# FNet and GeGLU block: the feature DFT for all tiles first, then the sequence DFT with its weights stationary, four of 16 chunks as block products

## Chip, cores and metric

One core of one Trainium2 chip. The metric is the device time in microseconds of one execution, as the median of several runs; 732.07 us for the kernel before (3 runs, 731.82 to 732.6).

## What is computed

```python
def _A_ref(x, dft_seq_re, dft_seq_im, dft_hid_re, dft_hid_im):
    a = jnp.einsum("bsd,ed->bse", x, dft_hid_re)
    b = jnp.einsum("bsd,ed->bse", x, dft_hid_im)
    y = jnp.einsum("ts,bse->bte", dft_seq_re, a) - jnp.einsum("ts,bse->bte", dft_seq_im, b)
    return y

def _B_ref(x, w_gate, w_up, w_down):
    g = jnp.einsum("bsd,df->bsf", x, w_gate)
    u = jnp.einsum("bsd,df->bsf", x, w_up)
    h = _gelu(g) * u
    return jnp.einsum("bsf,fd->bsd", h, w_down)

x = A_x
h = x + _A_ref(_layernorm(x, axis=-1), ...)
h2 = h + _B_ref(_layernorm(h, axis=-1), B_w_gate, B_w_up, B_w_down)
```

All tensors are fp32, with S = 2048 tokens, D = 448 features and 1792 hidden features; the batch is 1.

## The kernel before

Every fp32 operand of a matmul is split into two fp16 numbers, a hi half (rounded on ACT, `hi_part`, L105) and a lo half (the rest, on DVE, `lo_part`, L109 or L111). A product is three matmuls: hi x hi and the two mixed ones. TensorE has two sequencer records per matmul, the weight load (PEld: the stationary operand, 128 x 128) and the matmul (PE: the moving operand streams by, its columns are the width in the rows). PSUM has 8 banks of 512 fp32 columns.

The program has two stages, which run one after the other on PE.

*DFT stage.* It has 64 steps: 4 output blocks of 512 tokens (`b`) by 16 chunks of 128 input tokens (`c`). A tile of x is loaded (L340), normalised (`x_stats`, `x_norm`) and split (`xs`, kept on chip for all blocks). In a step `seq_mm` (L412) multiplies with the *x tile stationary* and the sequence DFT matrix `ws` moving, 512 columns: 2 parts (real, imaginary) x 3 feature slices x 3 terms = 18 matmuls into 6 banks; `seq_mm_rest` (L426) does the last 64 features of both parts in 6 half-width matmuls for a seventh bank. After 16 steps `z_out` splits the seven banks into `z`, and `hid_mm` (L477) applies the feature DFT: 4 token tiles x 7 slices x 3 terms = 84 matmuls of 448 columns; DVE adds x (L485) and gives `hx`, the h of the residual. For three blocks the `hid_mm` stand in between the steps of the next block; for the last they stand at its end. `w_seq` comes in 64 loads of 512 KB (L364), is split on ACT and DVE, five buffers ahead. In the same stage h of blocks 0 and 1 is normalised, split and transposed by DMA (`ffn_transpose`, L285) into `hops`, and the 14 gate/up weight blocks are summed, split (`class Weights`) and stored (`w_dram`, L333), the last three kept in a ring of buffers (`gw`).

*Gate/up and down stage.* 56 blocks of `GateUp` (L716, `product`, 256 columns, Strassen-like sums of operands) with the Gelu on ACT and products on POOL, and from block 14 on the down matmuls (L660, 224 columns). h of blocks 2 and 3 is prepared here. A last part does the remaining down matmuls without Gelu (L879, and L660 again).

The order is written out by hand and each engine runs its own file in that order: `early` and `after` hang work on a step of the DFT stage, `side` on a block of the second one. SP issues all DMAs in one file and waits there for what an issue needs.

Of the kernel before, what the change touches and what calls it, by code (L numbers as in the profile page):

```python
# [32 lines left out]
def kernel(  # L33
# [46 lines left out]
    ps_tr = ctx.enter_context(tc.tile_pool(name="ps_tr", bufs=1, space=bass.MemoryType.PSUM))  # L80
    right = ctx.enter_context(ExitStack())
    ps_seq = right.enter_context(tc.tile_pool(name="ps_seq", bufs=7, space=bass.MemoryType.PSUM))
# [6 lines left out]
    sign_t = const.tile([P, 1], F32, name="sign_t")  # L89
    G.memset(sign_t[:64], D_SC)  # L90
    G.memset(sign_t[64:], -D_SC)

# [4 lines left out]
    pw = ps_tr.tile([P, 8, P], F16, tag="tr", name="pw")  # L97
    for k in range(56):
        PE.transpose(pw[:, k % 8, :], ident, ident)  # L99
# [61 lines left out]
    def pair_tile(name):  # L161
        return ring.tile([P, 2, D], F32, tag="xh", bufs=5, name=name)

    def w_tile(name):
        return ring.tile([P, 28 * P], F16, tag="w", bufs=3, name=name)
# [125 lines left out]


    class Weights:


        def __init__(self, f):
            self.f = f
            self.raw = dft.tile([P, 2, 6, P], F32, tag="raw", bufs=2, name=f"gu_raw{f}")
            for r in range(2):
                nc.sync.dma_start(self.raw[:, r], w_gu[f, :, r])  # L300

        def sums(self):
            gate, up = self.raw[:, 0], self.raw[:, 1]
            s = self.s = dft.tile([P, 10, P], F32, tag="s", name=f"gu_s{self.f}")
            V.tensor_add(s[:, 0:3], up[:, 0:3], up[:, 3:6])
            V.tensor_sub(s[:, 3:6], s[:, 0:3], gate[:, 0:3])
            V.tensor_sub(s[:, 6:8], gate[:, 0:2], up[:, 0:2])
            V.tensor_sub(s[:, 8:10], gate[:, 4:6], s[:, 4:6])
# [15 lines left out]
        def split(self, of_raw):  # L324
            if of_raw:
                self.w = w_tile(f"gu_w{self.f}")
# [9 lines left out]
    xt, xs, norm_x = {}, {}, {}  # L336

    def x_load(i):
        xt[i] = dft.tile([P, 1, D], F32, tag="xt", bufs=3, name=f"x{i}")
        nc.sync.dma_start(xt[i][:, 0, :], x[i * P : (i + 1) * P, :])  # L340

    def x_stats(i):
        mv = stats(xt[i], f"x{i}")
        norm_x[i] = mv, root(mv, f"x{i}")

    def x_norm(i):
        mv, sd = norm_x.pop(i)
        xn = xt[i][:, 0, :]
        normed(xn, xn, mv, rstd(mv, sd, f"x{i}"), 0)
        xs[i] = dft.tile([P, 2, D], F16, name=f"xs{i}")  # L350
        hi_part(xs[i][:, 0], xn)

    def x_lo(i):
        lo_part(xs[i][:, 1], xt[i][:, 0, :], xs[i][:, 0])

    wr, ws = {}, {}

    def seq_load(n):
        wr[n] = dft.tile([P, 8 * P], F32, tag="wr", bufs=5, name=f"wr{n}")
        b, q, jj = n // NT, n // 2 % 8, n % 2
        nc.sync.dma_start(wr[n], w_seq[(2 * b + jj) * 8 + q])  # L364

    def seq_hi(n):
        if n % 2 == 0:
            ws[n // 2] = dft.tile([P, 2, 2, 8 * P], F16, tag="ws", bufs=4, name=f"ws{n // 2}")
        hi_part(ws[n // 2][:, 0, n % 2], wr[n], D_SC)

    def seq_lo(n):
        t = ws[n // 2][:, :, n % 2]
        lo_part(t[:, 1], wr[n], t[:, 0], D_SC)


    def first_load(c, jj):
        if c == 0:
            wr[jj] = dft.tile([P, 8 * P], F32, tag="wr", bufs=5, name=f"wr{jj}")
        if c == jj == 0:
            ws[0] = dft.tile([P, 2, 2, 8 * P], F16, tag="ws", bufs=4, name="ws0")  # L380
        cols = slice(c * P, (c + 1) * P)
        nc.sync.dma_start(wr[jj].rearrange("p (b t) -> p b t", b=4)[:, :, cols], w_seq[jj * 8][:, :, cols])

    def first_views(c, jj):
        cols = slice(c * P, (c + 1) * P)
        ts = [wr[jj], ws[0][:, 0, jj], ws[0][:, 1, jj]]
        return [t.rearrange("p (b t) -> p b t", b=4)[:, :, cols] for t in ts]

    def first_hi(c, jj):
        src, hi, lo = first_views(c, jj)  # L390
        hi_part(hi, src, D_SC)

    def first_lo(c, jj):
        src, hi, lo = first_views(c, jj)
        lo_part(lo, src, hi, D_SC)

    def seq_w(n, l, part):

        t = ws[n // 2][:, l].rearrange("p a (r g c t) -> p r c a g t", r=2, g=2, c=2)
        return t[:, part, n % 2]  # L400

    TERMS = ((0, 0), (1, 0), (0, 1))
    acc = {}

    def seq_mm(n, parts, terms=range(3)):

        b, c = divmod(n, NT)
        for part in parts:
            for k in range(3):
                for m in terms:  # L410
                    lx, lw = TERMS[m]
                    PE.matmul(  # L412
                        acc[b, 3 * part + k],
                        xs[c][:, lx, k * P : (k + 1) * P],
                        seq_w(n, lw, part),
                        start=c == 0 and m == 0,
                        stop=c == NT - 1 and m == 2,
                    )

    def seq_mm_rest(ns):  # L420

        for n in ns:
            b, c = divmod(n, NT)
            for m, (lx, lw) in enumerate(TERMS):
                for part in range(2):
                    PE.matmul(  # L426
                        acc[b, 6][64 * part : 64 * part + 64, :],
                        xs[c][:, lx, 3 * P :],
                        seq_w(n, lw, part),
                        start=c == 0 and m == 0,  # L430
                        stop=c == NT - 1 and m == 2,
                        skip_group_check=True,
                    )

    z = {}

    def z_out(b, k):
        if k == 0:
            z[b] = dft.tile([P, 2, 7, TB], F16, tag="z", name=f"z{b}")
        sc = 1.0 / (X_SC * D_SC)  # L440
        ps = acc.pop((b, k))
        hi_part(z[b][:, 0, k], ps, sc)
        lo_part(z[b][:, 1, k], ps, z[b][:, 0, k], sc)


    wh = dft.tile([P, 2, 7, D], F16, name="wh")
    wh_raw = {}

    def wh_load(g):

        t = wh_raw[g] = dft.tile([P, (3, 3, 1)[g], D], F32, tag="raw", bufs=2, name=f"wh_raw{g}")
        if g < 2:
            nc.sync.dma_start(t, w_hid[:, 0:3, g * D : (g + 1) * D])
        else:
            for r in range(2):
                nc.sync.dma_start(t[64 * r : 64 * r + 64, 0], w_hid[64 * r : 64 * r + 64, 3, r * D : (r + 1) * D])

# [683 lines left out]
```

## Time and profile before

| | us |
|---|---|
| median of 3 runs | 732.07 |
| profiled execution, span from first to last instruction | 730.1 |
| the runs' median less that span | 1.97 |
| first sequence matmul | 7.10 |
| first gate/up matmul | 364.91 |
| PE busy over the span | 718.5 |
| DVE, ACT, POOL busy | 523.0, 277.9, 242.1 |

The page holds one execution; its own time is the span beside what lies around it, which only the runs show. A row of a group reads: line, engine, operation, output <- input (partitions x elements, type) x count | busy us, mean ns of one | idle time of the engine just before, and what ended most of it. PE rows of a timeline include the pipelined end of the last matmul, so the distance of two starts, not the length of a row, is the price of what lies between; the pieces of the chain leave that end out.

### The profile page before, as it was taken

How to read it: one execution, taken by the hardware profiler on the slowest of the kernel's cores; microseconds unless marked ns; L12 is line 12 of the kernel's file. 1: busy time of each engine (PE TensorE's matmuls, PEld its weight loads, DVE VectorE, ACT ScalarE, POOL GpSimd, SP SyncE). 2: the span in 40 equal slices, each digit the busy share in tenths (PEclk: the TensorE clock that was granted, in tenths of full speed). 3: DMA queues.
4: the chain of work that ended last, by engine and by line, in shares of the span. 5: the costliest groups of instructions: out<-in, count | busy, mean ns of one | idle time of the engine just before them, and what ended most of it. 6: DMA issues, size and time to landing. Idle time of an engine off the chain costs nothing.

```text
span 730.1 us, 13452 instructions
## 1 busy us (share of the span) xinstructions
PE 718.5 (98%) x5309; PEld 497.9 (68%) x5309; DVE 523.0 (72%) x1071; ACT 277.9 (38%) x544; POOL 242.1 (33%) x281
## 2 busy tenths in 40 slices
PE   9999999999999999999999999999999999999987
PEld 5444444444444444444588889999999999999977
DVE  7888667486665866441377778787887877989794
ACT  4444703256233442311043444442444434454421
POOL 0000000000000001000057865576685867768360
PEclk9999999999999999999999999999999999999999
DMA  8667466577667976530057654747447676555311
GB/s 280 227 218 235 163 231 208 185 211 256 231 214 218 316 253 241 219 122 5 26 206 262 240 207 167 181 168 209 176 147 225 186 213 228 219 179 185 127 39 39
DMA packets 63503, 139.84 MB, mean 192 GB/s; under 512 B 30288, under 2 KB 39504, under 8 KB 63440
## 3 DMA queue, kind: packets, MB, share of 16 engines
q1 hardware_dynamic: 63440, 138.99, 57.2%
q8 instruction: 41, 0.67, 0.4%
q14 instruction: 22, 0.18, 0.1%
HBM read 112.23 MB, written 20.19 MB: 181 GB/s over the span
## 4 chain that ended last, share of the span: by engine, by line
PE 93%; DVE 4%; DMA 1%; ACT 1%; issue 1%; POOL 0%; POOLq 0%; DVEq 0%; ACTq 0%
PE acc L412 34%; PE pY L716 13%; PE acc_d L660 12%; PE y L477 9%; PE pZ L716 9%; PE pX L716 9%; PE acc L426 6%; DMA gw<-w_dram 1%; PE pw L99 1%; DVE last_v L900 1%; DVE last_a L109 1%; DVE last_s L904 1%; PE last_Y L879 1%; PE last_X L879 1%; DVE last_s L903 0%
## 5 line engine op out<-in xcount | busy, mean ns | idle before, releaser
L412 PE MATMUL acc<-ws,xs 128*128 128x512 f16 x1152 | 253.8, 379 | 0.0
L716 PEld LDWEIGHTS <-gw 128*128 128x128 f16 x2067 | 201.9, 98 | 24.1 <-issue 2.4
L412 PEld LDWEIGHTS <-xs 128*128 128x128 f16 x1152 | 111.3, 98 | 138.3 <-issue 6.5
L716 PE MATMUL pY<-hops,gw 128*128 128x256 f16 x901 | 123.0, 273 | 1.9 <-DVE u L726 1.7
L660 PE MATMUL acc_d<-wd,dn_w 128*128 128x224 f16 x882 | 105.1, 259 | 0.0
L203 POOL TENSOR_TENSOR wd_s<-wd 128x448 f32<-128x448 f32 x7 | 7.9, 1131 | 273.8 <-DVE gu_w L111 273.8
L111 DVE SCALAR_TENSOR_TENSOR ws<-wr,ws 128x1024 f16<-128x1024 f32 (+1 forms) x66 | 78.0, 1188 | 15.5 <-ACT ws L105 15.2
L105 ACT ACTIVATE ws<-wr 128x1024 f16<-128x1024 f32 (+1 forms) x66 | 66.3, 1021 | 57.3 <-DMA wr<-in_w_seq_dram 28.1
L660 PEld LDWEIGHTS <-dn_w 128*128 128x128 f16 x882 | 85.0, 98 | 2.9
L716 PE MATMUL pX<-hops,gw 128*128 128x256 f16 x583 | 81.0, 273 | 0.8 <-DMA gw<-w_dram 0.8
L716 PE MATMUL pZ<-hops,gw 128*128 128x256 f16 x583 | 79.2, 273 | 0.0
L783 POOL TENSOR_TENSOR hh<-hh,g 128x256 f32<-128x256 f32 x42 | 31.0, 738 | 143.9 <-DVE hh L726 142.8
L726 DVE SCALAR_TENSOR_TENSOR u<-pY,u 128x256 f32<-128x256 f32 x112 | 46.9, 419 | 27.4 <-ACT c L790 18.8
L485 DVE SCALAR_TENSOR_TENSOR hx<-y,hx 128x448 f32<-128x448 f32 x16 | 10.0, 625 | 77.8 <-PE y L477 77.8
L477 PE MATMUL y<-wh,z 128*128 128x448 f16 x336 | 65.7, 352 | 0.0
L754 ACT ACTIVATE u<-pX 128x256 f32<-128x256 f32 x56 | 21.4, 383 | 90.3 <-PE pX L716 90.2
L477 PEld LDWEIGHTS <-z 128*128 128x128 f16 x336 | 32.8, 98 | 31.6 <-issue 0.4
L109 DVE TENSOR_TENSOR dn_w<-dn_s,dn_w 128x640 f16<-128x640 f32 x42 | 53.0, 1261 | 1.6 <-ACT dn_w L105 1.2
L767 ACT ACTIVATE g<-pX 128x256 f32<-128x256 f32 x56 | 21.5, 384 | 74.3 <-PE pX L716 69.0
L792 POOL TENSOR_TENSOR hh<-hh,c 128x256 f32<-128x256 f32 x42 | 41.2, 981 | 17.2 <-ACT c L790 17.0
L426 PE MATMUL acc<-ws,xs 128*64 128x512 f16 x384 | 44.7, 381 | 0.0
L810 POOL TENSOR_TENSOR dn_s<-hh 128x256 f32<-128x256 f32 x42 | 43.4, 1034 | 0.0
(112 smaller groups left out, 829.4 us busy)
## 6 DMA issues: line engine op xcount, KB each, us to landing
gw<-w_dram SPq DMA_DIRECT2D x53, 896.0 KB, 4.8
wr<-in_w_seq_dram SPq DMA_DIRECT2D x62, 512.0 KB, 5.9
w_dram<-gu_w SPq DMA_DIRECT2D x14, 896.0 KB, 4.7
gu_raw<-in_w_gu_dram SPq DMA_DIRECT2D x28, 384.0 KB, 5.6
wd<-in_w_down_dram SPq DMA_DIRECT2D x14, 448.0 KB, 5.6
x<-in_x_dram SPq DMA_DIRECT2D x16, 224.0 KB, 2.8
hx<-in_x_dram SPq DMA_DIRECT2D x8, 448.0 KB, 6.7
h_dram<-hx SPq DMA_DIRECT2D x8, 448.0 KB, 2.7
```

Source lines behind the costliest of these rows:

```text
L105: A.activation(dst, src, AF.Copy, scale=scale)
L109: V.tensor_sub(dst, src, hi)
L111: V.scalar_tensor_tensor(dst, src, scale, hi, op0=ALU.mult, op1=ALU.subtract)
L412: PE.matmul(acc[b, 3 * part + k], xs[c][:, lx, k * P : (k + 1) * P], seq_w(n, lw, part), start=c == 0 and m == 0, stop=c == NT - 1 and m == 2,
L426: PE.matmul(acc[b, 6][64 * part : 64 * part + 64, :], xs[c][:, lx, 3 * P :], seq_w(n, lw, part), start=c == 0 and m == 0, stop=c == NT - 1 ...
L477: PE.matmul(y[:, :D], z[b][:, lz, k, i * P : (i + 1) * P], wh[:, lw, k, :], start=k == 0 and m == 0, stop=k == 6 and m == 2,)
L660: PE.matmul(acc[k // 2][:, k % 2 * HD : (k % 2 + 1) * HD], a_of(la, a), b_of(lb, b), start=first and m == 0 and k % 2 == 0, stop=last and ...
L716: PE.matmul(ps, w[:, wl, wa + ws, :], ops[:, m + ms, :], start=first and n == 0, stop=last and n == len(terms) - 1, skip_group_check=True,)
L726: V.scalar_tensor_tensor(dst, ps, SC, other, op0=ALU.mult, op1=ALU.add)
L783: G.tensor_mul(c21, c21, self.g1)
L792: G.tensor_mul(c22, c22, self.c12)
L810: G.tensor_sub(s[:, 2:4], t[:, 1:4:2], t[:, 0:4:2])
```

## The change

The two DFTs change places. First each of the 16 tiles of x goes through the feature DFT (`feature_mm`, 22 matmuls of 448 columns): the normalised tile's hi and lo halves (896 fp16 columns) are transposed into `xT`, the first four tiles by PE with a copy by ACT (`x_turn_pe`), the others by DMA (`x_turn`); the transposed tile is stationary and the feature matrix `wh_hi`, `wh_lo` moves. `feature_out` leaves the real and the imaginary part of the result in hi and lo halves on chip (`bop`).

Then the sequence DFT runs in eight passes p of 256 output tokens. A unit u is two of the 16 chunks; its piece of `w_seq` (512 KB, in two loads now) is split into `ws` and is *stationary*, `bop` moves. A plain unit has 24 matmuls of 448 columns into two banks; units 6 and 7 (four chunks) have sums of the operands formed (`seq_sums`, `feature_sums`) and seven block products of 224 columns with three terms each, 42 matmuls into all four banks of the pass. `seq_out` combines the four banks and adds x; passes alternate between two sets of four banks. The units of pass 0 stand between the feature tiles, as soon as their tiles are done. Slots 0 to 79 are the 16 feature tiles and 64 units in PE's order; `plan(n, rank, ...)` hangs the other engines' work ahead of slot n.

Besides: 50 warm-up transposes instead of 56; gate/up weight blocks have one raw buffer instead of two and are spread over all passes; the down weights' loads and sums move from the DFT stage into the next one, three blocks later; the pair ring `xh` has 4 buffers instead of 5; the Gelu table is loaded early; the moments of the last pair are taken in blocks 23 and 24.

```diff
-    def seq_mm(n, parts, terms=range(3)):
-        b, c = divmod(n, NT)
-        for part in parts:
-            for k in range(3):
-                for m in terms:
-                    lx, lw = TERMS[m]
-                    PE.matmul(
-                        acc[b, 3 * part + k],
-                        xs[c][:, lx, k * P : (k + 1) * P],
-                        seq_w(n, lw, part),
...
+    def x_turn(i):
+        xT_tile(i)
+        nc.sync.dma_start_transpose(xT[i], xs[i])
...
+        for k in range(k0, k1):
+            PE.transpose(ptr[i][:, k, :], xs[i][:, k * P : (k + 1) * P], ident)
+        A.activation(xT[i][:, k0:k1, :], ptr[i][:, k0:k1, :], AF.Copy)
...
+    def feature_mm(i, parts=range(2), tag="B"):
+        if 0 in parts:
+            feat[i] = [ps_dft.tile([P, 512], F32, tag=tag, name=f"ab{i}_{r}") for r in range(2)]
+        steps = [[], [(k, wh_lo, k) for k in range(4)]]
+        for k in range(4):
+            steps[0] += [(k, wh_hi, k)] + ([(4 + k, wh_hi, k)] if k < 3 else [])
+        for part in parts:
+            for n, (kx, w, kw) in enumerate(steps[part]):
+                for r in range(2):
+                    PE.matmul(
+                        feat[i][r][:, :D],
+                        xT[i][:, kx, :],
+                        w[:, kw, r * D : (r + 1) * D],
...
+            if is_s(u):
+                for a, o, k, half in PRODUCTS:
+                    for m, (lb, lw) in enumerate(TERMS):
+                        mm(k, slice(half * HD, half * HD + HD), w[:, lw, a, cc * P : (cc + 1) * P], b[:, lb, o], end and m == 2)
+            else:
+                for k, a0 in ((0, 2), (1, 0)):
+                    for r in range(2):
+                        for m, (lb, lw) in enumerate(TERMS):
+                            rhs = b[:, lb, 2 * r : 2 * r + 2].rearrange("p o d -> p (o d)")
+                            mm(k, slice(0, D), w[:, lw, a0 + r, cc * P : (cc + 1) * P], rhs, end and r == 1 and m == 2)
...
+    def seq_out(p):
+        X, Y, Z, W = acc.pop(p)[0]
+        h = hp[divmod(p, 2)]
+        e = fops.tile([P, 4, HD], F32, tag="tt", name=f"e{p}")
+        stt = V.scalar_tensor_tensor
+        A.activation(e[:, 1], Z[:, 0:HD], AF.Copy, scale=SC_Y)
+        stt(h[:, 0], X[:, 0:D], SC_Y, h[:, 0], op0=ALU.mult, op1=ALU.add)
+        stt(e[:, 0], W[:, 0:HD], -SC_Y, e[:, 1], op0=ALU.mult, op1=ALU.add)
...
+                plan(n - 3, 5, lambda i=c: x_norm(i), lambda i=c: x_lo(i))
+                plan(n - 2, 2, lambda i=c: x_turn(i))
...
+                plan(n + 1, 1, lambda i=c: feature_out(i))
...
+        plan(n - 2, 3, lambda p=p, u=u: seq_split(p, u))
...
+        plan(n, 1, lambda p=p: seq_out(p))
+        plan(n + 1, 5, lambda q=q, j=j: ffn_stats(q, j, hp[q, j]))
...
+    x_turn_pe(0, 0, 4)
+    wh_high(1)
+    x_turn_pe(0, 4, 7)
+    x_rstd(1)
+    x_norm(1)
+    wh_high(2)
+    wh_high(3)
+    wh_low(3, G)
+    x_stats(2, 3)
+    x_lo(1)
+    feature_mm(0, (0,))
+    x_turn_pe(1, 0, 4)
+    x_turn_pe(1, 4, 7)
```

ACT's file at the start of the program, before the change (`sd` is the root for a tile's deviation, `ws` the sequence matrix, `xs` the x tile's hi half):

```order
L126 ACTIVATE sd_x0_197<-mv_x0_193,eps_t_82 128x1
L105 ACTIVATE ws0_177<-wr0_176 128x4x128
L105 ACTIVATE ws0_177<-wr1_179 128x4x128
L105 ACTIVATE xs0_208<-x0_174 128x448
L126 ACTIVATE sd_x1_216<-mv_x1_212,eps_t_82 128x1
L105 ACTIVATE ws0_177<-wr0_176 128x4x128
L105 ACTIVATE ws0_177<-wr1_179 128x4x128
L105 ACTIVATE xs1_228<-x1_181 128x448
```

The same place after the change (`xT_ps` is the PSUM bank of PE's transposes, `wh_hi` the feature matrix):

```order
L121 ACTIVATE sd_x0_182<-mv_x0_178,eps_t_79 128x1
L100 ACTIVATE wh_hi_164<-wh_raw0_166 128x896
L100 ACTIVATE xs0_192<-x0_169 128x448
L121 ACTIVATE sd_x1_198<-mv_x1_194,eps_t_79 128x1
L370 ACTIVATE xT0_202<-xT_ps0_203 128x512
L100 ACTIVATE wh_hi_164<-wh_raw0_166 128x896
L370 ACTIVATE xT0_202<-xT_ps0_203 128x384
L100 ACTIVATE xs0_192<-x0_169 128x448
L100 ACTIVATE wh_hi_164<-wh_raw1_167 128x896 x2
L121 ACTIVATE sd_x2_233<-mv_x2_226,eps_t_79 128x2
L370 ACTIVATE xT0_202<-xT_ps1_253 128x512
L370 ACTIVATE xT0_202<-xT_ps1_253 128x384
```

The four pieces of the feature matrix and the copies of the transposed tiles stand in one file now, and the root for tiles 2 and 3 ahead of the copies of tile 1.

DVE's file where the DFT stage gives way to the first gate/up block, before (`hx` takes the last feature result from `y`, `u2_0` is the first sum of that block):

```order
L485 SCALAR_TENSOR_TENSOR hx3_1_3046<-y_3_3_3230,hx3_1_3046 128x448
L180 BN_STATS st_h3_1_1_3254<-hx3_1_3046 128x6
L181 BN_AGGR mv_h3_1_3226<-st_h3_1_1_3254 128x2
L726 SCALAR_TENSOR_TENSOR u2_0_3285<-pY_0_3270,u1_0_3283 128x256
L133 RECIPROCAL r_h3_1_3289<-sd_h3_1_3287 128x2
```

And after (the six rows of `seq_out` for the last pass, then the same sum):

```order
L518 SCALAR_TENSOR_TENSOR hx7_3675<-acc7_0_3566,hx7_3675 128x448
L519 SCALAR_TENSOR_TENSOR e7_3855<-acc7_3_3569,e7_3855 128x224
L520 SCALAR_TENSOR_TENSOR hx7_3675<-acc7_1_3567,hx7_3675 128x448
L521 SCALAR_TENSOR_TENSOR e7_3855<-acc7_3_3569,e7_3855 128x224
L522 SCALAR_TENSOR_TENSOR e7_3855<-acc7_2_3568,e7_3855 128x224
L523 SCALAR_TENSOR_TENSOR e7_3855<-acc7_2_3568,e7_3855 128x224
L858 SCALAR_TENSOR_TENSOR u2_0_3902<-pY_0_3887,u1_0_3900 128x256
```

Ahead of `u2_0` stood one drain and the moments of its tile; now six drains stand there, which read the banks of the last pass.

526 lines of the change are left out of this document (308 added, 218 removed).

## Prediction

> **What bounds the kernel now.** I read the page's busy times and chain first, then the stages, the groups by shape, and the chain and timelines of the places that change.
>
> ```profile
> span 730.1 us, 13452 instructions
> PE 718.5 (98%) x5309; PEld 497.9 (68%) x5309; DVE 523.0 (72%) x1071; ACT 277.9 (38%) x544; POOL 242.1 (33%) x281
> ...
> PE 93%; DVE 4%; DMA 1%; ACT 1%; issue 1%; POOL 0%; POOLq 0%; DVEq 0%; ACTq 0%
> ```
>
> PE is busy 98% and carries 93% of the chain. The change rewrites one stage, so I read that stage by itself: the window from the first sequence matmul (7.10) to the first gate/up matmul (364.91). Its columns are length, then busy us and count of PE, PEld, DVE, ACT and POOL, clock, DMA share, GB/s.
>
> ```profile
> 7.10:364.91 357.81, 357.77 (x1876) 164.41 (x1874) 228.32 (x480) 128.31 (x204) 2.84 (x3) 1.00 0.61 203
> ```
>
> In 357.81 us PE is idle for 0.04. So here a matmul less is time less, and any new wait of PE is time more. DVE is busy 64% of it, ACT 36%.
>
> **The matmuls: price by width.** Chain pieces (start, length) of the three old kinds, and timeline rows of a run of 84 matmuls of 224 columns, which ends where the row at 699.30 starts:
>
> ```profile
> 60.05 2.71 PE acc L426 x24
> 62.76 15.65 PE acc L412 x72
> ...
> 121.12 3.97 PE y L477 x21
> ...
> 349.07 16.00 PE y L477 x84
> ```
> ```profile
> 691.25 0.26 PE L879 MATMUL last_tr<-wd,h_last 128*128 128x224 f16 x1
> ...
> 699.30 0.74 PE L660 MATMUL acc_d<-wd,h_last 128*128 128x224 f16 x6
> 699.88 1.70 PE L660 MATMUL acc_d<-wd,last_a 128*128 128x224 f16 x15
> 701.42 0.74 PE L660 MATMUL acc_d<-wd,h_last 128*128 128x224 f16 x6
> ```
>
> 512 columns: 15.65/72 = 217.4 ns. 448 columns: 3.97/21 = 189.0 to 16.00/84 = 190.5; I take 189.5. 224 columns: (699.30 - 691.25)/84 = 95.8; I take that, because it is long and undisturbed. Removed: 1152 of L412, 384 of L426 and 336 of L477, which fill the 357.8. Added: 352 feature matmuls (22 per tile) and 8 passes x 12 chunks x 12 = 1152 sequence matmuls, all of 448 columns, so 1504 x 189.5 = 285.0; and 8 x 4 x 21 = 672 of 224 columns, x 95.8 = 64.4. Sum 349.4: **-8.4 us** if PE never waits. (By the ends of the 448 price: -9.1 to -6.9.) The four-chunk block products give little: as plain chunks they would be 384 x 189.5 = 72.8 instead of 64.4.
>
> Here the Trainium skill speaks against the change. Its page "TensorE: Matmul & The Clock Gate", section "LDWEIGHTS (loading the stationary operand)", gives a weight load P/1.2 ns, so 106.7 ns for 128 columns, which is longer than a 224-column matmul here. By that rule a narrow matmul would be spaced 106.7 and the 672 would take 71.7, so 7.3 us more. The trace disagrees, with 84 of them at 95.8; what is left of the rule is a rival below.
>
> **The start.** Before, the first tile goes this way, and then PE runs without a gap:
>
> ```profile
> 3.22 0.63 DVE L119 BATCH_NORM_STATS2 st_x<-x 128x6 f32<-128x448 f32 x1 [3.22 <-DMA x<-in_x_dram]
> 5.21 0.51 DVE L142 TENSOR_SCALAR x<-x,mv_x,r_x 128x448 f32<-128x448 f32 x1
> 6.04 0.56 ACT L105 ACTIVATE xs<-x 128x448 f16<-128x448 f32 x1
> 7.10 7.93 PE L412 MATMUL acc<-ws,xs 128*128 128x512 f16 x36
> ```
>
> Afterwards a feature matmul needs a *transposed* tile (PE transposes, ACT copies out of PSUM in two parts) and wh_hi. ACT does all of it in one file, by these groups (mean ns after the bar):
>
> ```profile
> L105 ACT ACTIVATE ws<-wr 128x1024 f16<-128x1024 f32 x62 | 63.8, 1046 | 56.5 <-DMA wr<-in_w_seq_dram 27.4 <-PE acc L426 21.9 <-issue 7.1
> L105 ACT ACTIVATE z<-acc 128x512 f16<-128x512 f32 x28 | 16.7, 598 | 34.5 <-PE acc L412 25.1 <-PE acc L426 8.5
> L105 ACT ACTIVATE xs<-x 128x448 f16<-128x448 f32 x16 | 9.2, 577 | 32.9 <-DVE x L142 32.8
> L224 ACT ACTIVATE xn_h<-hx,nb_h,r_h 128x448 f32<-128x448 f32 x8 | 5.7, 754 | 2.3 <-DVE nb_h L222 2.2
> L109 DVE TENSOR_TENSOR xs<-x,xs 128x448 f16<-128x448 f32 x16 | 9.7, 604 | 1.0 <-ACT xs L105 1.0
> ```
>
> On the line through these, 896 columns (wh_high) take 0.94, the 512 and 384 of a copy 0.60 and 0.50. ACT: hi of x0 at 5.72 to 6.3, copy 7.2 to 7.8, wh_high(1) to 8.74, second copy to 9.24, hi of x1 to 9.8, wh_high(2) and (3) to 11.68. Feature 0's last hi matmul needs wh_high(3), so it ends near 12.15, where 14 x 189.5 from 7.1 would have ended at 9.75: +2.4. Then each of tiles 1, 2 and 3 is transposed just ahead of its use, and PE stands behind it in order: 4 transposes, copy (0.60), 3 transposes that wait for that copy, and in tiles 1 and 2 the second feature pair waits for the second copy (0.50). With 0.15 per hand-over that is about 1.75, 1.7 and 1.45. The third tile's statistics stand ahead of x1's lo on DVE and wait for the seventh load, 2.75 MB after the start:
>
> ```profile
> 3.00:4.00 1.00, 1.00 (x12) 1.00 (x10) 0.74 (x2) 0.00 (x0) 0.00 (x0) 1.00 0.99 280
> ...
> 10.00:11.00 1.00, 1.00 (x7) 0.41 (x6) 0.95 (x3) 0.40 (x1) 0.00 (x0) 1.00 1.01 406
> ```
>
> The first tile (229 KB) landed at 3.2; the other 2.52 MB take 6.2 us at 406 GB/s and 9.0 at 280, so they land at 9.4 to 12.2. I take 9.7, since these rows are as long as those that ran at 406; it then hides behind ACT. At 12.2 it costs 2 us more. Sum of the start: **+7.3** (the 66 matmuls of three tiles end at 26.9 instead of 19.6), from 4.1 (only the first two terms) to 9.3.
>
> **The fill.** x4 is the first tile that SP turns by DMA. On DVE its statistics stand behind the drains of features 0 and 1, whose hi halves stand behind tile 3's copies on ACT: statistics near 27.8, hi and lo to 32.9. The first sequence unit's lo half is done near 31.95, where PE arrives at 31.1 and needs it two matmuls later: +0.4. The turn then lands by this row
>
> ```profile
> hops<-xs SPq DMA_TRANSPOSE x32, 5.8
> ```
>
> at 38.8; the queue is empty by then, so perhaps from 37. PE arrives at 36.1: +0.9 to +2.7, I take 1.8. Together **+2.2**. From then on a pair of tiles and a unit take PE 2 x 4.17 + 4.55 = 12.9 us, and each turn stands two slots ahead of its use (over 8 us), so I count nothing more; the cover is gone if DVE or ACT falls over 2 us behind.
>
> **The passes.** DVE's prices here:
>
> ```profile
> L111 DVE SCALAR_TENSOR_TENSOR ws<-wr,ws 128x1024 f16<-128x1024 f32 x62 | 75.3, 1221 | 15.5 <-ACT ws L105 15.2 <-DMA wr<-in_w_seq_dram 0.3
> L111 DVE SCALAR_TENSOR_TENSOR gu_w<-gu_s,gu_w 128x512 f16<-128x512 f32 x28 | 18.0, 685 | 0.0
> L485 DVE SCALAR_TENSOR_TENSOR hx<-y,hx 128x448 f32<-128x448 f32 x16 | 10.0, 625 | 77.8 <-PE y L477 77.8
> L623 DVE SCALAR_TENSOR_TENSOR hr<-acc_d,hr 128x224 f32<-128x224 f32 x28 | 10.2, 384 | 2.6 <-PE acc_d L660 2.3
> ```
>
> A line through the first two is 149 ns + 1.05 per column. A pass is 6 x 24 x 189.5 + 2 x 42 x 95.8 = 35.3 us of PE. DVE in it: six plain units 7.3, the block units' sums and lo halves 7.4, the drain seq_out 2 x 0.625 + 4 x 0.384 = 2.8, moments 2.4, gate/up weights 2.2 of 14 blocks at 4.4 = 9.9, and in passes 0 to 3 the split of h, about 5: **34.8 of 35.3**. But two lo halves back to back take less than twice the mean:
>
> ```profile
> 15.70 2.35 DVE L111 SCALAR_TENSOR_TENSOR ws<-wr,ws 128x1024 f16<-128x1024 f32 x2
> ```
>
> so 1.175 each, and some 33.5 in all. Each lo half is queued two slots (9 us) before PE needs it; adding the durations up slot by slot, DVE is at most 4.3 us behind, in passes 1 and 2. I count **+0.5** (0 to 6). ACT does the hi halves of the same operands at 0.84 ns per column (the two rows of 1046 and 598), so about four fifths of DVE's lo halves and none of the sums; POOL adds e to h twice per pass. Neither is a bound. DMA needs 512 KB per 4.5 us.
>
> **The hand-over.** Before, u2 of the first gate/up block is ready in time:
>
> ```profile
> 366.53 0.41 DVE L726 SCALAR_TENSOR_TENSOR u<-pY,u 128x256 f32<-128x256 f32 x1
> ```
> ```profile
> 364.91 0.82 PE L716 MATMUL pX<-hops,gu_w 128*128 128x256 f16 x6
> ...
> 367.42 0.82 PE L716 MATMUL pY<-hops,gu_w 128*128 128x256 f16 x6
> ```
>
> PE needs it 2.5 us after the block begins. Afterwards the last seq_out (2.8) stands ahead of it: 0.2 + 2.8 + 0.4 = 3.4, so PE waits **+0.9**. Everything behind (364.91 to 730.1) I leave as it is: the down weights are prepared three blocks later, still ten ahead of their use; the moments of the last pair (1.6 us) move into blocks 23 and 24, where DVE has room (72% busy over the span); the early load of the Gelu table and the six warm-up transposes fewer hide under PE's own work or the load of x.
>
> **Sum:** -8.4 + 7.3 + 2.2 + 0.5 + 0.9 = +2.5 on the profiled span, so 732.6. The median of the runs shown, 732.07, lies 1.97 above the span of 730.1; with the same distance the forecast is **734.6**.
>
> **Rivals.**
> - *The start is cheap.* Only the first two start terms count (+4.1), the turns land in time: -8.4 + 4.1 + 0.5 + 0.9 = -2.9, so 729.2. For it: DMA has 406 GB/s to give, and the hand-overs of 0.15 are my reading. Against: ACT's file is long whatever the loads do. 0.30.
> - *DVE becomes the bound of passes 1 to 4* (the slower side): from 35.3 us of demand per pass, which 34.8 plus some waits for ACT and for the single gate/up raw buffer would pass. At 1.5 us over per pass, +6: 740.6. Against: the 1.175 above. 0.11.
> - *Narrow matmuls cost more.* The row of 15 gives (701.42 - 699.88)/15 = 102.7; 672 x 6.9 ns = +4.6: 739.2. Against: it waited for last_a at that place. 0.05. By the Trainium skill's weight-load rule of the page above the time would be 741.9, an estimate.
> - *PE falls back to its first rate at the start.* The 56 warm-up transposes took
>
> ```profile
> 1.37 5.89 PE L99 MATMUL pw<-ident 128*128 128x128 f16 x56 [1.37 <-POOL sign_t L90]
> 704.49 1.42 PE L660 MATMUL acc_d<-wd,last_a 128*128 128x224 f16 x13 [2.14 <-DVE last_a L109]
> ```
>
> 105 ns each, twice the 54 that 128 columns cost later. Between 6.6 and 12.2 PE would work less than half the time; if 28 feature matmuls ran at half rate, +5.3: 739.9. Against: after the idle 2.14 us at 704.49 the 13 matmuls took 1.42, so full rate. The Trainium skill's page "TensorE: Matmul & The Clock Gate", section "Part 1: The HAM clock gate", says that an idle window of about 3.4 us halves the clock; no gap that I foresee is so long, and no gap in this trace tests it. 0.06.
>
> **How the numbers follow.** The forecast has 0.48 (own range 731 to 738). Within 0.2% of the median, about what a measurement here can tell from no change, is 730.6 to 733.5. Faster: most of the first rival, 0.28. Same: parts of it and of the forecast, 0.15. Slower: 0.57. The range 727 to 742 takes in a start of 4.1 without other waits and the dear rivals.
>
> **What would show it.** Right: PE's first feature matmul near 8, three gaps of over a microsecond behind xT copies before 20, slot 3 near 27, a wait for a DMA turn near 36, passes of 35.3 without idle, and the gate/up stage beginning near 366.5. Wrong: PE waits for ws in the passes; the first U after 33; spacing of 224 columns above 100 ns; a granted clock under 1.00 at the start; or an unbroken PE from 12 on, which would make the change faster.

## The result, and the profile after

The changed kernel takes **741.07 us** (median of 4 runs, 739.75 to 742.56) where the kernel before takes 731.98 on the same chip: a ratio of 1.012, 95% interval 1.0103 to 1.0138. The forecast was 734.6, so the sign was right and the time is inside the range, but the change costs 9.1 us and not 2.5. The profiled execution of the changed kernel took 740.13, its span is 738.3; before it was 730.1.

The head of the page after, and the shares of its chain:

```profile
span 738.3 us, 14480 instructions
...
PE 714.9 (97%) x5635; PEld 545.3 (74%) x5635; DVE 577.0 (78%) x1135; ACT 320.7 (43%) x601; POOL 286.2 (39%) x310
...
PE 74%; DVE 12%; DMA 6%; ACT 4%; issue 2%; POOL 2%; SPq 0%; DVEq 0%; ACTq 0%; POOLq 0%
```

PE works 3.6 us less than before, and its share of the chain falls from 93% to 74%: others now decide stretches of the time. Which stretches, the timeline of PE at the change of stage says first. Columns: start, length, engine, line, then output <- inputs, and what PE waited for.

```profile
363.71 3.00 PE L491 MATMUL acc<-b,ws 128*128 128x448 f16 x15
366.55 0.82 PE L848 MATMUL pX<-hops,gu_w 128*128 128x256 f16 x6
367.21 0.82 PE L848 MATMUL pY<-hops,gu_w 128*128 128x256 f16 x6
...
369.06 0.82 PE L848 MATMUL pY<-hops,gu_w 128*128 128x256 f16 x6
```

The first gate/up matmul starts at 366.55, where the forecast had 366.5 and the kernel before 364.91: the rewritten stage is only 1.64 us longer. The other 6.6 us lie behind it, where the same matmuls run as before. To find them, take one instruction that occurs once in each of the 56 gate/up blocks, ScalarE's copy of the first product (`u1`), and subtract its start times in the timelines of two kernels:

| us from one `u1` copy to another | before | after |
|---|---|---|
| start of the span to block 0 | 365.82 | 367.41 |
| block 0 to 13 | 56.59 | 56.90 |
| **block 13 to 17** | **25.17** | **30.92** |
| block 17 to 26 | 56.43 | 56.43 |
| **block 26 to 27** | **6.27** | **7.09** |
| block 27 to 55 | 175.56 | 175.56 |

From block 0 to 55 the stage is 6.9 longer, and two places hold 6.57 of it: +5.75 in blocks 13 to 16 and +0.82 in block 26. Blocks 0 to 12 give 0.31 more; all other blocks agree to 0.01 us. What follows block 55 is 0.3 shorter. The same stretch (`u1` of block 13 to that of block 17) as a window, before and after; columns as in the prediction, so DVE is the third pair of numbers, POOL the fifth:

```profile
422.41:447.58 25.17, 23.95 (x225) 21.88 (x225) 20.62 (x44) 9.44 (x24) 15.17 (x17) 1.00 0.47 170
```
```profile
424.31:455.23 30.92, 24.80 (x230) 22.11 (x228) 26.82 (x47) 12.29 (x27) 22.59 (x23) 1.00 0.43 154
```

PE's matmuls are nearly the same, but DVE has 6.2 us more work and POOL 7.4 more. DVE's 26.8 alone would not have fitted into the 25.17 of before. That gives 1.65 at least; the stretch grew by 5.75, nearly all that DVE's work grew by, because DVE's idle time there was not filled: it is 4.10 after and was 4.55 before. The longest waits of PE in this stage after (total, times, longest), and the four waits in blocks 14 to 16:

```profile
PE pY L848 <- DVE u L858: 5.7, 5, 2.3
PE acc_d L791 <- DVE last_a L104: 3.9, 4, 2.1
PE pX L848 <- DMA gw<-w_dram: 1.7, 3, 0.7
PE pY L848 <- DVE hh L858: 0.9, 2, 0.6
```
```profile
436.80 0.71 PE L848 MATMUL pY<-hops,gw 128*128 128x256 f16 x5 [2.28 <-DVE u L858]
439.62 0.82 PE L848 MATMUL pY<-hops,gw 128*128 128x256 f16 x6 [0.64 <-DVE hh L858]
445.58 0.71 PE L848 MATMUL pY<-hops,gw 128*128 128x256 f16 x5 [1.56 <-DVE u L858]
453.00 0.71 PE L848 MATMUL pY<-hops,gw 128*128 128x256 f16 x5 [1.00 <-DVE u L858]
```

These four sum to 5.48. Before, waits for `u` cost PE 1.7 in the whole stage. What stands ahead of the late `u` at 436.32, on DVE and on POOL after:

```profile
432.70 1.49 DVE L106 SCALAR_TENSOR_TENSOR wd<-wd_s,wd 128x1120 f16<-128x1120 f32 x1
434.12 0.94 DVE L104 TENSOR_TENSOR dn_w<-hh,dn_w 128x256 f16<-128x256 f32 x1
435.58 0.83 DVE L104 TENSOR_TENSOR dn_w<-dn_s,dn_w 128x640 f16<-128x640 f32 x1 [0.52 <-ACT dn_w L100]
436.32 0.42 DVE L858 SCALAR_TENSOR_TENSOR u<-pY,u 128x256 f32<-128x256 f32 x1
...
437.12 1.11 DVE L943 TENSOR_TENSOR dn_s<-hh 128x128 f32<-128x128 f32 x1
438.15 1.08 DVE L217 SCALAR_TENSOR_TENSOR nb_h<-mv_h,r_h 128x2 f32<-128x2 f32 x1
```
```profile
436.96 1.12 POOL L198 TENSOR_TENSOR wd_s<-wd 128x448 f32<-128x448 f32 x1
438.05 1.18 POOL L200 TENSOR_TENSOR wd_s<-wd 128x448 f32<-128x448 f32 x1
```

`wd` and `wd_s` are the down weights and their sums, `dn_w` and `dn_s` the same of the hidden features that they are multiplied with. Before, the weights were ready when block 14 began the down matmuls; prepared three blocks later, their last halves fall into the first blocks that also split `dn_w`.

### The profile page after: what moved, and what is told of

It is laid out like the page before. It is cut to its first block, busy times and chain, and to the rows that moved or that the text cites. A ratio compares the mean times of both kernels' runs of the same rounds, so it can differ in the third digit from the quotient of the medians.

```text
span 738.3 us, 14480 instructions
## 1 busy us (share of the span) xinstructions
PE 714.9 (97%) x5635; PEld 545.3 (74%) x5635; DVE 577.0 (78%) x1135; ACT 320.7 (43%) x601; POOL 286.2 (39%) x310
## 4 chain that ended last, share of the span: by engine, by line
PE 74%; DVE 12%; DMA 6%; ACT 4%; issue 2%; POOL 2%; SPq 0%; DVEq 0%; ACTq 0%; POOLq 0%
PE acc L491 27%; PE pY L848 12%; PE acc_d L791 11%; PE ab L404 8%; PE pX L848 8%; PE pZ L848 7%; DMA gw<-w_dram 3%; DVE ws L106 2%; DMA wr<-in_w_seq_dram 1%; DVE dn_w L104 1%; DMA gu_raw<-in_w_gu_dram 1%; DVE last_v L1032 1%; DMA x<-in_x_dram 1%; DVE last_a L104 1%; ACT ws L100 1%
## 5 line engine op out<-in xcount | busy, mean ns | idle before, releaser
L491 PE MATMUL acc<-b,ws 128*128 128x448 f16 (+1 forms) x1824 | 283.9, 318 | 0.7 <-DVE ws L106 0.7
L491 PEld LDWEIGHTS <-ws 128*128 128x128 f16 x1824 | 176.8, 98 | 107.0 <-DVE ws L106 2.1
L525 POOL TENSOR_TENSOR hx<-hx,e 128x448 f32<-128x448 f32 x16 | 25.2, 1594 | 259.3 <-DVE e L522 199.3
L106 DVE SCALAR_TENSOR_TENSOR ws<-wr,ws 128x1024 f16<-128x1024 f32 x64 | 79.3, 1239 | 25.4 <-ACT ws L100 19.3
L100 ACT ACTIVATE ws<-wr 128x1024 f16<-128x1024 f32 x64 | 63.6, 997 | 66.9 <-PE acc L491 44.4
L404 PEld LDWEIGHTS <-xT 128*128 128x128 f16 x352 | 34.3, 99 | 34.7 <-ACT xT L370 2.1
L915 POOL TENSOR_TENSOR hh<-hh,g 128x256 f32<-128x256 f32 x42 | 35.8, 853 | 57.7 <-DVE hh L858 57.7
L404 PE MATMUL ab<-wh_hi,xT 128*128 128x448 f16 x224 | 46.9, 360 | 1.4 <-DMA xT<-xs 1.0
L941 POOL TENSOR_TENSOR dn_s<-hh 128x256 f32<-128x256 f32 x42 | 43.5, 1035 | 0.0
L942 POOL TENSOR_TENSOR dn_s<-hh 128x256 f32<-128x256 f32 x42 | 43.1, 1026 | 0.0
L782 POOL TENSOR_TENSOR hr<-hr,v 128x224 f32<-128x224 f32 x48 | 40.0, 853 | 0.0
```

The lines of the kernel that those rows point to most:

```text
L100: A.activation(dst, src, AF.Copy, scale=scale)
L106: V.scalar_tensor_tensor(dst, src, scale, hi, op0=ALU.mult, op1=ALU.subtract)
L404: PE.matmul(feat[i][r][:, :D], xT[i][:, kx, :], w[:, kw, r * D : (r + 1) * D], start=part == 0 and n == 0, stop=part == 1 and n == 3,)
L491: PE.matmul(banks[k][:, cols], lhs, rhs, start=k not in begun, stop=stop, skip_group_check=True)
L782: op(x, x, m)
L941: G.tensor_add(s[:, 0:2], t[:, 0:2], t[:, 2:4])
```

## Theories

**A:** the three-block delay of the down weights costs the 5.75. **B:** the moments of the last pair, moved from the change of stage into blocks 23 to 25, cost the 6. **C:** the gate/up weight loads, now with a third buffer in another pool, come late (PE's waits for the loads of `gw`: 1.7 after, 0.8 before). A second question is whether the terms of the DFT stage were right one by one, or only their sum.

All runs, each against the kernel before on the same chip:

| kernel | median us | ratio to before, 95% interval |
|---|---|---|
| the change | 741.07 | 1.0120 (1.0103 to 1.0138) |
| e1_unshift | 735.72 | 1.0044 (1.0031 to 1.0057) |
| e2_moments | 743.52 | 1.0161 (1.0144 to 1.0179) |
| e3_before_shift | 736.97 | 1.0072 (1.0054 to 1.0089) |
| e4_one_unit | 743.25 | 1.0153 (1.0135 to 1.0171) |
| e5_two_ps | 733.10 | 1.0015 (1.0006 to 1.0024) |
| e6_fill | 734.36 | 1.0026 (1.0014 to 1.0037) |
| e7_three | 746.64 | 1.0196 (1.0178 to 1.0213) |
| e8_three_pool | 766.52 | 1.0465 (1.0443 to 1.0488) |
| e9_all | 733.11 | 1.0014 (1.0004 to 1.0025) |
| e10_three_early | 749.74 | 1.0251 (1.0232 to 1.0269) |
| e11_catchup | 753.84 | 1.0302 (1.0283 to 1.0321) |
| e12_shift1 | 735.88 | 1.0062 (1.0039 to 1.0084) |

## Experiment 1: the delay undone, and the delay alone

e1_unshift is the changed kernel without the delay. The two tags are exchanged because `tt` is in use until the last `seq_out`.

```diff
-        wd32[n] = fops.tile(..., tag="xn" if n % 2 else "tt", ...)
+        wd32[n] = fops.tile(..., tag="tt" if n % 2 else "xn", ...)
...
+    plan(66, 9, lambda: down_load(0))
+    plan(70, 9, lambda: down_sums(0))
...
-    down_load(0)
...
+        if t <= 2 * NC:
+            down_prep(t)
...
-            if t == 2:
-                down_sums(0)
-            if t > 2:
-                down_prep(t - 3)
...
-        if t - 3 <= 2 * NC:
-            down_prep(t - 3)
```

> The changed kernel with the down weights prepared again from block 0 of gate/up (their first load and sums in the last pass of the sequence DFT, as before the change), instead of three blocks later. Theory A, the three blocks' delay pushes the halves and sums of the down weights into blocks 14 to 17, where the down projection has begun and VectorE has no room: blocks 14 to 17 lose their +5.7, and the time falls from 741.1 to 735.4 (734.5 to 736.5). Theory B, the moments of the last pair (moved into blocks 23 and 24) cost it: no change, 741. Theory C, the third gate/up buffer in a pool of its own makes the weight loads late (waits of TensorE for gw of 1.7 in all): no change either, 740 to 741.

e3_before_shift puts the same delay into the kernel before:

```diff
-    at(early, 56, lambda: down_sums(0))
...
-        if t <= 2 * NC:
-            down_prep(t)
+        if q > 0 and t - 3 <= 2 * NC:
+            down_prep(t - 3)
...
+            if t == 2:
+                down_sums(0)
+            if t > 2:
+                down_prep(t - 3)
```

> The kernel before the change, with one thing of the change: the down weights prepared three blocks later in gate/up (the first sums in block 2). Theory A: +5.7 on the kernel before, 737.7 (736.5 to 738.7), with the step in blocks 14 to 17. Theories B and C: no change, 732.0.

e1 is 735.72, and e3 736.97: by the ratios, 0.76 points under the change (5.6 us) and 0.72% over the kernel before (5.3 us), both inside the ranges of theory A. The window from `u1` of block 13 to that of block 17, of e1 and then of e3:

```profile
425.62:450.77 25.15, 23.94 (x225) 21.85 (x225) 20.59 (x44) 9.41 (x24) 15.13 (x17) 1.00 0.48 169
```
```profile
422.80:453.80 31.00, 25.85 (x225) 22.78 (x225) 26.27 (x47) 12.40 (x27) 22.67 (x23) 0.94 0.44 156
```

Undoing the delay restores 25.15, and the delay alone makes 31.00 of it in a kernel that has nothing else of the change. The same stretch takes 31.00 and 30.99 in e2 and e4 below, which keep the delay, and 25.16 to 25.17 in e5 to e10, which do not. TensorE's granted clock is no rival: it is 0.94 in e3's stretch and 1.00 in the change's, and the times agree. Theory A is shown both ways; B and C expected no change in either. In e1's profiled execution the first `u1` comes at 368.70, 1.29 later than in the change, which experiment 4 takes up.

## Experiment 2: the moments put back

```diff
+    ffn_stats(NB - 1, 1, hp[NB - 1, 1])
...
-    for g in range(2):
-        at(side, (23 + g, 1), lambda g=g: ffn_moments(NB - 1, 1, hp[NB - 1, 1], g))
-    at(side, (25, 4), lambda: ffn_rstd(NB - 1, 1))
```

> The changed kernel with the moments of the last pair computed where they stood before, ahead of gate/up, the down weights still three blocks late. Theory A: only the step of +0.8 at block 28 goes, 740.3, or nothing where VectorE's moments stand in the way of the first blocks' u2 (741). Theory B: the whole +6, 735. Theory C: no change.

743.52, 0.41% dearer than the change: all three expectations missed. Its step from block 26 to 27 is 6.27 again, so the 0.8 there came with the moved moments and their square root. But the first `u1` comes at 371.82 instead of 367.41. ScalarE in e2 at the change of stage, and PE behind it:

```profile
371.61 0.30 ACT L121 ACTIVATE sd_h<-mv_h,eps_t 128x2 f32<-128x2 f32 x1 [13.85 <-DVE mv_h L176]
371.82 0.36 ACT L886 ACTIVATE u<-pX 128x256 f32<-128x256 f32 x1
372.20 1.28 ACT L1130 ACT_TABLE_LOAD   x1
```
```profile
368.12 0.82 PE L848 MATMUL pZ<-hops,gu_w 128*128 128x256 f16 x6
372.23 1.23 PE L848 MATMUL pX<-hops,gu_w 128*128 128x256 f16 x5 [3.29 <-ACT u L886]
```

The square root waits for the moments, these for the last `seq_out`, and `u1` is queued behind the square root on ScalarE; PE waits 3.29; right behind this wait the granted clock is 0.50 for 3.4 us (372.2 to 375.6), which slows the next matmuls. Moving the moments was right here: of the 4.41 at the first `u1`, 0.26 lie ahead of the stage and 0.69 are made up by block 13, so it saves some 3.5 and costs 0.8; the medians differ by 3.0. ScalarE, after, around the moved square root:

```profile
509.13 1.28 ACT L121 ACT_TABLE_LOAD   x1
510.43 0.30 ACT L121 ACTIVATE sd_h<-mv_h,eps_t 128x2 f32<-128x2 f32 x1
511.66 0.38 ACT L886 ACTIVATE u<-pX 128x256 f32<-128x256 f32 x1 [0.94 <-PE pX L848]
512.07 1.28 ACT L922 ACT_TABLE_LOAD   x1
```

A root between two Gelus takes two table loads of 1.28; `c` and the `dn_w` halves stand behind the second. The Trainium skill's page "ScalarE: Activation LUTs", section "What ACT_TABLE_LOAD costs", gives about 1283 ns for one; the rows agree. PE waits twice here: 0.22 at 516.52 for a `u` that stands behind those halves on DVE, and 0.27 at 511.90 for an `hh` that stands behind the root's five small operations on DVE. So the tables are part of the 0.8; how large a part, no run separates.

## Experiment 3: the price of the block products

```diff
-    S_UNITS, WR = (6, 7), 3
+    S_UNITS, WR = (7,), 3
```

> The changed kernel with one unit of two chunks as block products instead of two (the other as plain products of 448 columns). By the matmuls' durations of the profile before (a plain unit 24 at 189.5 ns = 4.55, a unit of block products 42 at 95.8 ns = 4.02) the eight passes are 8 x 0.52 = 4.2 longer: 745.3. If VectorE bounds the passes instead, its lighter unit gives that back: 741 to 742. If narrow matmuls cost more than their columns on this chip, by the 106.7 ns that a weight load took, the plain unit costs next to nothing: 741.7.

743.25, between the first expectation and the two others; against the change +0.33%, 2.4 us, and the two intervals overlap, so the medians alone do not decide between 4.2 and 0.6. The rows do. A plain unit and a unit of block products in the changed kernel, each from its start to the start of the next row:

```profile
46.22 4.70 PE L491 MATMUL acc<-b,ws 128*128 128x448 f16 x24
50.76 0.54 PE L404 MATMUL ab<-wh_hi,xT 128*128 128x448 f16 x2
```
```profile
80.27 4.19 PE L491 MATMUL acc<-b,ws 128*128 128x224 f16 x42
84.30 0.92 PE L404 MATMUL ab<-wh_hi,xT 128*128 128x448 f16 x4
```

4.54/24 = 189.2 ns and 4.03/42 = 96.0 ns: the forecast's 189.5 and 95.8. A price of 106.7 ns for a narrow matmul is excluded. In e4 the first gate/up matmul starts at 369.38 instead of 366.55, +2.8. Of the 1.4 that are missing to 4.2, 0.5 is a wait for `ws` at 216.68 that the change has and e4 has not, and 0.4 lies ahead of the feature tile at 42.05 (41.69 in e4); the rest I did not find.

## Experiment 4: the start

e5_two_ps is e1 with a PSUM tile for each part of a transpose; e6_fill is e1 with 28 transposes of the identity in PE's gaps.

```diff
-        if k0 == 0:
-            xT_tile(i)
-            ptr[i] = ps_dft.tile([P, 8, P], F16, tag="A", name=f"xT_ps{i}")
+        if k0 == 0:
+            xT_tile(i)
+        ptr[i] = ps_dft.tile([P, 8, P], F16, tag="A", name=f"xT_ps{i}_{k0}")
```

> The kernel of e1_unshift, and at the start each part of a transpose on TensorE (four blocks, then three) gets a PSUM tile of its own, so that the second part does not wait for ScalarE's copy of the first. If these waits (0.69 each, before tiles x1, x2 and x3 in the trace of the changed kernel) lie on the path of the start, 0.7 to 2.1 go: 734.3 (733.6 to 735.0). If the start is bound by the transfers of the first loads and by VectorE, the waits only change their name: 735.7.

```diff
+    def fill(n):
+        for k in range(n):
+            PE.transpose(pw[:, k % 8, :], ident, ident)
...
     x_turn_pe(0, 0, 4)
+    fill(8)
...
     x_turn_pe(0, 4, 7)
+    fill(4)
...
     feature_mm(0, (0,))
+    fill(6)
     x_turn_pe(1, 0, 4)
+    fill(5)
...
     x_turn_pe(2, 0, 4)
+    fill(5)
```

> The kernel of e1_unshift with 28 more transposes of the identity on TensorE, in the gaps of the start from 6.8 to 19, so that TensorE is hardly idle there. The theory that sparse work of TensorE halves its granted clock for some 3.5 us at the start (0.50 from 9 to 12.5 in the changed kernel's profile, where it lay under the late second tile; 0.62 in 16 to 20 in e1_unshift's, where it made slot 3 start at 29.1 instead of 27.7): the clock stays at 1.00, slot 3 starts at 27.7, the profiled span is 732.4 and the median 734.3 to 735.7. Rival: the fillers themselves stand in front of the transposes, +0.3 to +1.

e5 takes 0.29% less than e1, 2.1 us: the waits for the copy were on the path. That is the upper end of the 0.7 to 2.1 expected, and 733.10 lies under the range of times. The profiled executions show less of it: the feature tile 3 (slot 3) starts at 26.47 in e5, and at 27.38 to 27.62 where a kernel with the change's start kept its full clock (e12, e2, e4). For e6 the clock is the question, and here it is in windows of PE (length, busy, clock, DMA share, GB/s) of the changed kernel, of e1 and of e6:

```profile
6.00:9.00 3.00, 0.78 (x9) 0.95 0.98 363
9.00:12.00 3.00, 3.00 (x10) 0.50 1.04 385
```
```profile
12.00:16.00 4.00, 2.22 (x15) 0.95 1.09 354
16.00:20.00 4.00, 3.46 (x13) 0.62 0.58 184
```
```profile
6.00:9.00 3.00, 1.95 (x21) 1.00 0.99 377
9.00:12.00 3.00, 2.85 (x19) 1.00 1.05 391
12.00:16.00 4.00, 3.33 (x27) 1.00 1.10 353
16.00:20.00 4.00, 3.39 (x27) 1.00 0.54 172
```

In the change the clock fell to 0.50 between 9 and 12, in e1 it fell after 15, and in e6's profiled execution, with the gaps filled, not at all. That the fillers keep it up is not shown: it did not fall in e2, e4, e5 and e12 either, whose gaps are open, and three of e6's ten executions have a mean clock of 0.997 to 0.998. Where it falls matters more than that it falls. In the change, PE would have waited for tiles 1 and 2 anyway: the statistics of tiles 2 and 3, which stand ahead of tile 1's lo half on DVE, wait for the load of x until 11.61. At full clock in e4 PE waits for tile 1 until 12.92 and for tile 2 until 17.48, and slot 3 starts at 27.62; in the change, at 27.70. In e1 slot 3 starts at 29.11. In e6 it starts at 26.53, earlier than the 27.7 expected; the median 734.36 is as expected, 0.18% under e1's (1.3 us), but the intervals overlap. Nor do the medians hang on the clock: e1's four executions with a mean clock of 1.00 took 733.39 to 736.15, its four others 734.66 to 736.13.

e9_all joins e1, e5 and e6 and moves the moments again, into blocks 4 to 6:

```diff
-        at(side, (23 + g, 1), lambda g=g: ffn_moments(NB - 1, 1, hp[NB - 1, 1], g))
-    at(side, (25, 4), lambda: ffn_rstd(NB - 1, 1))
+        at(side, (4 + g, 6), lambda g=g: ffn_moments(NB - 1, 1, hp[NB - 1, 1], g))
+    at(side, (6, 6), lambda: ffn_rstd(NB - 1, 1))
...
+            do(t, 6)
```

> All that the runs so far point to, with the change's two units as block products: down weights from block 0 (e1_unshift), a PSUM tile for each part of a transpose (e5_two_ps), the 28 fillers at the start (e6_fill), and the moments of the last pair in blocks 4 and 5 with their square root in block 6, ahead of the down projection, instead of blocks 23 to 25. If the two table loads of ScalarE around that square root (1.28 each in the trace of the changed kernel) cost the 0.8 of block 27 because ScalarE has no room there, and has room in block 6: 0.8 less than e5_two_ps by this, and 0 to 0.7 less by the fillers: 731.9 (731.3 to 732.8), level with the kernel before. If they cost as much in block 6: 732.5 to 733.3.

733.11, as the second expectation has it and the same as e5 alone: the fillers and the second move add nothing that can be measured. The step from block 26 to 27 is 6.27 again, so the 0.8 left that place, but the median did not get shorter by it; blocks 0 to 13 took 57.62 in the profiled execution, 57.21 in e5's, so part of it may have come back there. With 1.0014 (1.0004 to 1.0025) e9, like e5 with 1.0015, comes to within about 1 us of the kernel before, and neither beats it.

## Experiment 5: a third unit of block products

e7_three is e1 with `S_UNITS` of (3, 6, 7); e8_three_pool also gives the sums of the sequence weights to POOL (three lines like the one shown); e10_three_early is e9 with three units, the sums a slot earlier and the gate/up weights pushed toward the last passes.

```diff
-    S_UNITS, WR = (6, 7), 3
+    S_UNITS, WR = (3, 6, 7), 3
...
-        V.tensor_add(s[:, 2], s[:, 0], r[:, 2])
+        G.tensor_add(s[:, 2], s[:, 0], r[:, 2])
```
```diff
-            plan(n - 3, 6, lambda p=p, u=u: seq_sums(p, u))
+            plan(n - 4, 6, lambda p=p, u=u: seq_sums(p, u))
...
-    at_f = [n0 + k * (len(slots) - 3 - n0) // NF for k in range(NF)]
+    at_f = [n0 + int((len(slots) - 3 - n0) * (k / NF) ** 0.85) for k in range(NF)]
```

> The kernel of e1_unshift with a third unit of two chunks as block products (unit 3 beside 6 and 7). If TensorE sets the passes: 8 x 0.52 = 4.2 less, 731.5 (730.8 to 732.5). If VectorE becomes the bound with its 2.4 more in each pass (it is 97% busy in 250 to 285 already): 733.5 to 737.

> The kernel of e7_three with the sums of the sequence weights on GpSimd instead of VectorE. If VectorE bounds some passes of e7_three, 0.5 to 3 less than e7_three; if not, the same as e7_three within 0.5; if GpSimd's work slows VectorE's by sharing, as in blocks 14 to 17 of the changed kernel (a product of 0.28 took 1.11 there), 1 to 4 more.

> The kernel of e9_all with three units of block products, their sums on VectorE made one slot earlier, and the gate/up weights spread less on the passes that also carry the operands of gate/up and more on the last three. If e7_three lost its 11 to the order (ScalarE waiting 55 in all for the sums on VectorE, and VectorE for ScalarE), most of it comes back and TensorE's 4.2 show: 728 to 731. If VectorE's work itself is too much (91 to 96% busy in the passes of e7_three): 736 to 745.

All three missed on the dear side: 746.64, 766.52 and 749.74. The waits of PE in e7 up to block 7 of gate/up, and two windows of 35 us in its passes:

```profile
PE acc L491 <- DVE ws L106: 10.6, 18, 2.0
PE ab L404 <- DMA xT<-xs: 2.7, 2, 2.1
```
```profile
75.00:110.00 35.00, 30.14 (x202) 19.16 (x201) 27.12 (x40) 19.31 (x29) 11.67 (x9) 1.00 0.34 85
180.00:215.00 35.00, 31.88 (x227) 21.32 (x225) 32.49 (x62) 15.66 (x25) 3.20 (x2) 1.00 0.88 245
```

PE waits for `ws` 18 times where the change waited twice (0.7). This is the forecast's rival "DVE becomes the bound", one unit further on. But in the first window no engine is full, so DVE's throughput is not the whole cause there; the chain from sums (DVE) to hi halves (ACT) to lo halves (DVE) is the other candidate. e8 speaks for the chain: with the sums on POOL, DVE is busy 23.59 of the first window and 31.79 of the second, less than in e7, yet PE waits 23.8 for `ws`. There the first sum of a unit takes 2.11 us on POOL, 0.94 on DVE, and ACT waits 76.5 in all for the sums instead of 55.5. Making the sums earlier did not help in e10, which also moved the gate/up weights and shows no effect of either alone. Which of the two decides in each pass was not separated.

## Experiment 6: late, but finished in time

e11_catchup keeps the late begin and does two steps a block from block 8; e12_shift1 is e1 one block later.

```diff
-            if t > 2:
-                down_prep(t - 3)
+            for s in range(t - 3, t - 2) if t < 8 else range(2 * t - 11, 2 * t - 9):
+                if 0 <= s < 2 * NC:
+                    down_prep(s)
...
-        if t - 3 <= 2 * NC:
-            down_prep(t - 3)
```

And in e12, in place of e1's line for block t:

```diff
+        if 0 < t <= 2 * NC + 1:
+            down_prep(t - 1)
```

> The changed kernel with the down weights still begun three blocks late (first sums in block 2, first halves in block 3), but two steps a block from block 8 on, so that the last halves stand in block 12, ahead of the down projection. Theory A in its sharper form, only the coincidence with the down projection's own work in blocks 14 to 17 costs: the step from block 13 to 17 is 25.2 as before instead of 30.9, and the time is that of e1_unshift, 735.4 to 736.5, where two steps fit into a block of 4.2. Rival, beginning late is what costs (buffers and loads later everywhere): 740 to 741.

> The kernel of e1_unshift with the down weights one block later instead of three, so that one step (the low halves of the last block's weights, about 1.3 to 1.5 on VectorE and nothing on ScalarE or GpSimd) falls into block 14. If each step that falls into blocks 14 to 16 costs a third of the 5.75: 737.6, and block 13 to 17 takes 27.1. If VectorE takes it in its gaps (it was 20.6 busy of 25.2 there) and the 5.75 need the chain of GpSimd's sums, ScalarE's high halves and VectorE's low halves in one block: 735.7 to 736.3 and 25.2 to 25.8.

e11 takes 753.84, over both expectations, and so decides for neither: by block 13 it has lost 16.1 (73.02 from block 0 to 13 instead of 56.90). ScalarE, ahead of the `u1` of blocks 10 and 11:

```profile
414.80 1.14 ACT L100 ACTIVATE wd<-wd_s 128x1120 f16<-128x1120 f32 x1 [5.82 <-POOL wd_s L201]
...
416.41 0.37 ACT L886 ACTIVATE u<-pX 128x256 f32<-128x256 f32 x1
...
422.66 1.14 ACT L100 ACTIVATE wd<-wd_s 128x1120 f16<-128x1120 f32 x1 [5.41 <-POOL wd_s L201]
```

My pairing put POOL's sums directly ahead of ScalarE's halves of them; ScalarE waits 5.3 to 6.1 a block, four times, with `u1` queued behind. That shows how dear one badly placed step is, not whether a late begin alone costs. From block 13 to 17 e11 takes 27.19, 2.0 over the 25.2 expected, though no step is left there; I did not find why.

e12's median is 735.88, in ratio 1.3 us over e1 with overlapping intervals. It fits the second expectation, but its interval takes in the first one's 737.6 too. Its profiled execution takes 28.25 from block 13 to 17, above both and 3.1 more than e1; as its `u1` of block 13 came early, it is 2.4 more from block 0 to 17. DVE is busy 23.54 in that stretch, 2.95 more than in e1. So wherever steps fall there, the stretch grew by about what DVE's busy time grew by (3.10 for 2.95 here, 5.75 for 6.20 in the change, 5.83 for 5.65 in e3), and 4.1 to 4.7 of DVE's time stayed idle. Whether DVE's sum of work makes it so or the order, the steps standing ahead of `u`, was not tried apart.

## Why the prediction was right in sign and short in size

The sign and the beginning of gate/up at 366.55 (forecast 366.5) came out, the latter by luck in part: the start was 0.8 dearer and the fill 1.0 cheaper than forecast, and the hand-over, which was to cost 0.9 behind it, cost nothing. That 741.07 lies inside 727 to 742 is luck as well. The upper end was drawn for rivals at 739.2 to 740.6 (DVE as the bound, narrow matmuls, the clock), and none of them made the time.

- *Matmuls, -8.4:* right; 189.2 and 96.0 ns.
- *Start, +7.3:* slot 3 at 27.70 where 26.9 was forecast, so +8.1. The waits behind the xT copies of tiles 1 to 3 were 0.69 each, not over a microsecond, and the third stood at 26.02, not before 20; e5 shows that they cost. The clock did fall, as the rival at 0.06 had it, and tile 0's 14 hi matmuls took 4.15 instead of 2.65; but slot 3 came 0.1 later than in e4, instead of 5.3, because PE would have waited for tiles 1 and 2. The load of x that I took at 9.7 ended a wait at 11.61, near my upper bound.
- *Fill, +2.2:* 1.15. The first unit waited 0.17, and the wait for a DMA turn was 0.98, at 42.05 and not near 36.
- *Passes, +0.5:* 0.53, at 216.68. Right; e7 shows that one more unit of block products does not fit.
- *Hand-over, +0.9:* nothing. The last `seq_out` begins while the last matmuls still run, and pY at 369.06 starts without a wait. With these terms the sum is +1.4 where the stage became 1.64 longer.
- **The step that failed:** "Everything behind (364.91 to 730.1) I leave as it is: the down weights are prepared three blocks later, still ten ahead of their use". The term was 0 and measured +5.75, shown by undoing it and by doing it alone. I checked the step against its consumer, ten blocks away, and not against what the engines do at its new time. In blocks 13 to 16 DVE was 20.6 of 25.17 busy; 6.2 more do not fit, and what cost was not only the 1.65 that do not fit: DVE's idle time stayed.
- The same sentence put the moments where "DVE has room (72% busy over the span)". At their new place the moments and their root cost 0.8, with two table loads on ScalarE and five small operations ahead of an `hh` on DVE. An average over the span says nothing about a block.

## What to carry to other kernels

A step that is moved costs what it displaces at its new place: look up that window's busy time engine by engine, add the step, and compare it with the window's length, even if its result is needed much later. What does not fit is a floor (1.65 here); where the engine's idle time lies between operations that others wait for, the whole added work can come on top (5.75 for 6.20). Take one instruction that recurs in every block and subtract its times between two traces: two numbers then say where a loss lies, which a total of waits does not. And what an edit moves along the way (here the down weights) can cost more than the edit's own subject; e1 avoids the delay with an exchange of two buffers.

## What the hardware showed that I had not expected

- DVE's small operation `nb_h` (2 columns) took 1.08 us at 438.15, where before it took 0.15; it ended with POOL's sum of 438.05 to 439.23. `dn_s` (128 columns) took 1.11 at 437.12, to just past the end of POOL's sum of 436.96 to 438.08, where it took 0.28 before in a quiet place and 0.81 beside a POOL operation. Both read two operands from SBUF. So DVE's time beside a busy POOL cannot be taken from a quiet place.
- TensorE's clock halved without a long idle stretch. In the change PE was busy 0.78 of the 3 us before, with no gap over 1.3; in e4 it was as sparse in 12 to 16 (2.23 of 4) as e1 (2.22), and only e1's clock fell. After the same wait in block 14 the clock fell in e3 (2.28, up to 435.27) and not in the change (2.28, up to 436.80). Four such falls last 3.4 us each: 8.7 to 12.1 in the change, 15.6 to 19.0 in e1, 372.2 to 375.6 in e2, 436.0 to 439.4 in e3. The Trainium skill's page "TensorE: Matmul & The Clock Gate", section "Part 1: The HAM clock gate", names a free-running window of 3413 ns; that the fall comes in one run and not in another agrees with it, its condition of an idle window does not.
